# Decay and bonus rows on another queue, the bonus turned earlier, and two parts of the weights placed later on GpSimd

## The chip, the cores and the metric

One core of a Trainium2 chip. The metric is the device time of the whole kernel in microseconds, lower is better. A run counts as slow when it is over 1.5% above the fastest of the same kernel.

## The reference

An RWKV-style attention with decay `w` and bonus `u`, followed by a SiLU feed-forward over all tokens.

```python
# batch 4, heads 8, seq 768, head_dim 48
for t in range(S):
    cur = einsum('bhd,bhe->bhde', u[None] * kt, vt)
    y[:, :, t] = einsum('bhd,bhde->bhe', rt, state + cur)
    state = w[None, :, :, None] * state + einsum('bhd,bhe->bhde', kt, vt)
# x = y as 3072 x 384
h = x @ w_in              # 384 x 2048
g = h * (1 / (1 + exp(-h)))
return g @ w_out          # 2048 x 384
```

## The kernel before

The sequence is cut into chunks of 128 tokens. A unit is one chunk of one batch row, so there are 24 units. For each unit r and k are transposed and multiplied by powers of the decay ("rk"), their products give the scores ("ae", "ao"), masked on VectorE ("am"), and these with v give y. The bonus of a token is the row sum of r k u ("rku") times v ("vu"), added to y. The feed-forward products of one chunk ("hps", then "ops") fill TensorE between the units of the next. What the change touches is the start:

```python
    load_row(wrow, w)                           # on SP's queue
    load(0, mid=lambda: load_row(urow, u))      # u ahead of v of unit 0
    for i in range(1, B): load(i)
...
    spin(5)                                     # products on zeros, to raise TensorE's clock
    wT = to_cols(wrow, None)                    # the decay turned into a column
    spin(4)
    # ... powers of the decay on VectorE: pif
...
    p1(0, mid=to_cols_u)       # unit 0: transposes, rk; the bonus turned inside
    ...
    nc.gpsimd.tensor_copy(out=gate, in_=rin[1][:, 0, 0:1])   # GpSimd waits for r of unit 1
    win_part(0, 512)           # first quarter of w_in, GpSimd's queue
    nat_ku(0); nat_rk(0)       # GpSimd: k*u, r*k*u of unit 0
    p2(0)                      # scores of unit 0
    p1(1, spins=1)
    bonus_sum(0)               # VectorE: row sum rku
    nat_ku(1); nat_rk(1); nat_v(1)
    p3y(0)
    bonus_act(0)               # ScalarE: eight products vu
    ...
    win_part(512, 1024)
    bonus_sum(1); bonus_vu(1)
    p2(1, spins=2)
    p3e(0)                     # y16 = y + vu
    ...                        # two more quarters follow behind unit 2's bonus
```

Of the kernel before, what the change touches and what calls it, by code (L numbers as in the profile page):

```python
# [15 lines left out]
def kernel(  # L16
# [11 lines left out]
    nc = tc.nc  # L28

    B, H, S, D = r.shape  # L30
# [5 lines left out]
    PR = 64 + D  # L36
# [14 lines left out]
    rin = [big.tile([128, H, 64], FP, name=f"rin{i}") for i in range(NIN)]  # L51
    kin = [big.tile([128, H, 64], FP, name=f"kin{i}") for i in range(NIN)]
    vin = [big.tile([128, H, D], FP, name=f"vin{i}") for i in range(NIN)]
# [7 lines left out]
    def unit(i):  # L61
        return divmod(i, B)

    def load(i, mid=None):
        if i >= NU:
            return
        sc, b = unit(i)
        for t, src in ((rin, r), (kin, k), (vin, v)):
            if t is vin and mid:
                mid()  # L70
            nc.sync.dma_start(out=t[i % NIN][:, :, 0:D],
                              in_=src[b, :, sc * C:sc * C + C, :]
                              .rearrange("h t d -> t h d"))
# [4 lines left out]
    urow = cst.tile([NP, 2, 64], FP)  # L78
# [3 lines left out]
        nc.vector.memset(t[:, :, D:64], 1.0)  # L82

    def load_row(t, src):
        nc.sync.dma_start(out=t[:, :, 0:D], in_=bass.AP(tensor=src.tensor, offset=0,
                                                        ap=[[PW, NP], [D, 2], [1, D]]))

    load_row(wrow, w)
    load(0, mid=lambda: load_row(urow, u))
    for i in range(1, B):  # L90
        load(i)
    for t in (rin, kin):
        nc.vector.memset(t[0][:, :, D:64], 0.0)
# [6 lines left out]
        out=maskM, in_=maskM, compare_op=ALU.is_ge, fill=0.0,  # L100
# [17 lines left out]
    def spin(n, t=None):  # L118

        if t is None:  # L120
            t = ps.tile([128, 512], FP, name="spin", tag="t", bufs=5)
        else:
            t = t.rearrange("s p t -> s (p t)")
        for _ in range(n):
            nc.tensor.matmul(t, junk[:, 0:128], junk, start=True, stop=True)

    def to_cols(row, copy):
        t = ps.tile([128, 512], FP, name="cols", tag="t", bufs=5)
        nc.tensor.transpose(t[0:PR, 0:NP], row.rearrange("p j d -> p (j d)")[:, 0:PR],
                            ident[0:NP, 0:NP])  # L130
        if copy is None:
            return t[0:PR, 0:NP]
        c = cst.tile([PR, NP], FP, name="cols_sb")
        copy(out=c, in_=t[0:PR, 0:NP])
        return c

    spin(5)
    wT = to_cols(wrow, None)
    spin(4)
    u_bc = cst.tile([128, H, D], FP)  # L140
    lamC = cst.tile([128, H, D], FP)

    def to_rows(dst, cols):

        t = ps.tile([128, NP, 2, 64], FP, name="rows", tag="t", bufs=5)
        for p in range(NP):
            nc.tensor.transpose(t[:, p, :, :].rearrange("t j d -> t (j d)")[:, 0:PR],
                                cols(p), ident[0:PR, 0:PR])
        nc.scalar.copy(out=dst.rearrange("t (p j) d -> t p j d", j=2), in_=t[:, :, :, 0:D])


    nc.vector.tensor_copy(out=pi[:, 0:NP, 1:2], in_=wT.unsqueeze(2))
# [2 lines left out]
    while n < C:  # L155
        nc.vector.tensor_tensor(
            out=pi[:, :, 1 + n:1 + 2 * n], in0=pi[:, :, 1:1 + n],
# [14 lines left out]
    def nat_v(i):  # L172
        L = live.setdefault(i, {})
        L["v16"] = wrk.tile([128, H, D], F16, name="v16", bufs=6)
        nc.scalar.copy(out=L["v16"], in_=vin[i % NIN])

    def nat_ku(i):
        L = live.setdefault(i, {})
        L["ku"] = wrk.tile([128, H, D], FP, name="ku")
        nc.gpsimd.tensor_tensor(out=L["ku"], in0=kin[i % NIN][:, :, 0:D], in1=u_bc,  # L180
                                op=ALU.mult)

    def nat_rk(i):
        L = live[i]
        L["rku_f"] = wrk.tile([128, H, D], FP, name="rku_f")
        nc.gpsimd.tensor_tensor(out=L["rku_f"], in0=rin[i % NIN][:, :, 0:D], in1=L["ku"],  # L186
                                op=ALU.mult)
# [6 lines left out]
    def bonus_sum(i):  # L194
        L = live[i]
        L["rku"] = wrk.tile([128, H], FP, name="rku", bufs=3)
        nc.vector.tensor_reduce(out=L["rku"], in_=L["rku_f"], axis=mybir.AxisListType.X,  # L197
                                op=ALU.add)

    def bonus_vu(i):  # L200
        L = live[i]
        L["vu"] = wrk.tile([128, H, D], FP, name="vu", bufs=3)
        nc.gpsimd.tensor_tensor(out=L["vu"], in0=vin[i % NIN],  # L203
                                in1=L["rku"].unsqueeze(2).broadcast_to([128, H, D]),
                                op=ALU.mult)
# [5 lines left out]
            nc.scalar.activation(out=L["vu"][:, h, :], in_=vin[i % NIN][:, h, :],  # L211
                                 func=AF.Copy, scale=L["rku"][:, h:h + 1])

    def p1(i, mid=None, spins=0):
        n = i % NIN
        L = live.setdefault(i, {})
        tr = ps.tile([128, NP, C], FP, name="tr", tag="t", bufs=5)
        tk = ps.tile([128, NP, C], FP, name="tk", tag="t", bufs=5)
        spin(spins, tr)
        for t, src in ((tr, rin), (tk, kin)):  # L220
            flat = src[n].rearrange("p h d -> p (h d)")
            for p in range(NP):
                nc.tensor.transpose(t[0:PR, p, :], flat[:, 128 * p:128 * p + PR], ident)
        rk = wrk.tile([PR, 2, NP, C], FP, name="rk")
        L["rT"] = rk[:, 0]
        nc.vector.tensor_tensor(out=L["rT"], in0=tr[0:PR], in1=lamR, op=ALU.mult)
        if mid:
            mid()
        L["kT"] = rk[:, 1]
        nc.vector.tensor_tensor(out=L["kT"], in0=tk[0:PR], in1=lamK, op=ALU.mult)  # L230

    def p1t(i):

        n = i % NIN
        L = live.setdefault(i, {})
        xs = [ps.tile([128, 2, NP, 64], FP, name="xs", tag="t", bufs=5) for _ in range(2)]
        for a, src in enumerate((rin, kin)):
            flat = src[n].rearrange("p h d -> p (h d)")
            for p in range(NP):
                for g in range(2):  # L240
                    t = slice(64 * g, 64 * g + 64)
                    nc.tensor.transpose(xs[g][0:PR, a, p, :],  # L242
                                        flat[t, 128 * p:128 * p + PR], ident[t, t])
        rk = wrk.tile([PR, 2, NP, C], FP, name="rk")
        L["rT"] = rk[:, 0]
        L["kT"] = rk[:, 1]
        L["xs"] = xs, rk

    def p1d(i):
        L = live[i]  # L250
        xs, rk = L["xs"]
        for g in range(2):
            nc.vector.tensor_tensor(out=rk[:, :, :, 64 * g:64 * g + 64], in0=xs[g][0:PR],  # L253
                                    in1=lam(g), op=ALU.mult)
# [6 lines left out]
    def p2(i, spins=0, nxt=None, late=False):  # L261
        L = live[i]
        ae = ps.tile([128, NP, C], FP, name="ae", tag="t", bufs=5)
        ao = ps.tile([128, NP, C], FP, name="ao", tag="t", bufs=5)
        spin(spins, ae)
        for p in range(NP):
            nc.tensor.matmul(ae[:, p, :], L["kT"][0:D, p, :], L["rT"][0:D, p, :],  # L267
                             start=True, stop=True)
            nc.tensor.matmul(ao[:, p, :], L["kT"][64:PR, p, :], L["rT"][64:PR, p, :],  # L269
                             start=True, stop=True)  # L270
        if nxt is not None:
            p1t(nxt)
        L["am"] = []
        for a in (ae, ao):
            am = wrk.tile([128, NP, C], F16, name="am", bufs=4)
            nc.vector.tensor_tensor(out=am, in0=a,  # L276
                                    in1=maskM.unsqueeze(1).broadcast_to([128, NP, C]),
                                    op=ALU.mult)
            L["am"].append(am)
        if nxt is not None and not late:  # L280
            p1d(nxt)
# [15 lines left out]
    def p3e(i):  # L297
        L = live[i]
        L["y16"] = wrk.tile([128, H, D], F16, name="y16", bufs=3)
        nc.vector.tensor_tensor(out=L["y16"], in0=L["y"], in1=L["vu"], op=ALU.add)  # L300
# [105 lines left out]
            f()  # L406


    def to_cols_u():
        t = to_cols(urow, nc.scalar.copy)  # L410
        to_rows(u_bc, lambda p: t[:, p:p + 1].broadcast_to([PR, 128]))

    zero = junk[0:PR, 0:HD].rearrange("r (p c) -> r p c", p=NP)
    gate = cst.tile([128, 1], FP)

    def win_part(c0, c1):
        nc.gpsimd.dma_start(out=win[:, :, c0:c1],
                            in_=moe_w_in[:, c0:c1].rearrange("(q p) n -> p q n", p=128))
# [4 lines left out]
            in_=moe_w_out[1024 * g:1024 * g + 1024, :].rearrange("(f p) n -> p f n", p=128))  # L423


    p1(0, mid=to_cols_u)
    nat_v(0)
    lamCT = cst.tile([PR, NP, C], FP)
    for p in range(NP):
# [1 line left out]
                             scale=pi[:, p, C:C + 1])  # L431

    nc.scalar.copy(out=st[0], in_=zero)
    nc.gpsimd.tensor_copy(out=gate, in_=rin[1][:, 0, 0:1])
    win_part(0, 512)
    nat_ku(0)
    nat_rk(0)
    p2(0)
    p1(1, spins=1)
    bonus_sum(0)  # L440
# [4 lines left out]
    to_rows(lamC, lambda p: lamCT[:, p, :])  # L445
    bonus_act(0)
    nc.scalar.copy(out=st[1], in_=zero)
    win_part(512, 1024)
    bonus_sum(1)
    bonus_vu(1)  # L450
    p2(1, spins=2)
    p3e(0)
    spin(4)
# [183 lines left out]
```

## Time and profile before

| | before |
|---|---|
| median of the first 3 runs | 197.83 us (197.67 to 198.09) |
| the profiled execution | 197.53 us, span 195.8 us |
| TensorE busy | 188.7 us, 96% of the span |
| first feed-forward product (hps) | 16.80 us from the start |
| gaps of TensorE from 40 us to the last output | none to speak of |

A span runs from the first to the last instruction on the core; the device time is about 1.7 us longer. A line of the timeline has start, duration, engine, source line, operation, output and inputs; the bracket at its end tells how long the engine was idle before and which instruction released it. The lines themselves stand in the prediction.

### The profile page before, as it was taken

How to read it: one execution, taken by the hardware profiler on the slowest of the kernel's cores; microseconds unless marked ns; L12 is line 12 of the kernel's file. 1: busy time of each engine (PE TensorE's matmuls, PEld its weight loads, DVE VectorE, ACT ScalarE, POOL GpSimd, SP SyncE). 2: the span in 40 equal slices, each digit the busy share in tenths (PEclk: the TensorE clock that was granted, in tenths of full speed). 3: DMA queues.
4: the chain of work that ended last, by engine and by line, in shares of the span. 5: the costliest groups of instructions: out<-in, count | busy, mean ns of one | idle time of the engine just before them, and what ended most of it. 6: DMA issues, size and time to landing. Idle time of an engine off the chain costs nothing.

```text
span 195.8 us, 4923 instructions
## 1 busy us (share of the span) xinstructions
PE 188.7 (96%) x1919; PEld 126.9 (65%) x1919; DVE 115.4 (59%) x233; ACT 91.0 (46%) x207; POOL 115.2 (59%) x145
## 2 busy tenths in 40 slices
PE   7789999899999999999999999999999999999993
PEld 2657878787767887675657656557656556544563
DVE  6687658885857775975486676467566344210121
ACT  3655487799212534216871025692025680069300
POOL 4499959979975779678668737834537710000000
PEclk9999999999999999999999999999999999999999
DMA  4999998999893684476456377626551011210022
GB/s 85 215 187 169 196 205 175 183 190 204 167 218 104 158 177 88 100 174 154 90 107 127 110 177 159 127 40 122 128 155 44 20 22 44 93 48 0 3 82 80
DMA packets 89696, 24.12 MB, mean 123 GB/s; under 512 B 82888, under 2 KB 89672, under 8 KB 89672
## 3 DMA queue, kind: packets, MB, share of 16 engines
q1 hardware_dynamic: 85992, 20.66, 48.5%
q0 software_dynamic: 3680, 3.15, 10.7%
q8 instruction: 15, 0.25, 0.5%
q14 instruction: 9, 0.07, 0.1%
HBM read 20.45 MB, written 4.72 MB: 129 GB/s over the span
## 4 chain that ended last, share of the span: by engine, by line
PE 87%; DVE 4%; issue 4%; POOL 3%; ACT 0%; POOLq 0%; DVEq 0%
PE ops L370 31%; PE hps L358 31%; PE ae L267 11%; PE xs L242 4%; PE y L293 3%; DVE am L276 2%; PE y L290 2%; PE sps L309 2%; PE ops L384 1%; POOL rku_f L186 1%; POOL ku L180 1%; PE yT L346 1%; PE ao L269 1%; DVE y L300 1%; DVE rku L197 1%
## 5 line engine op out<-in xcount | busy, mean ns | idle before, releaser
L361 ACT ACTIVATE gT<-hps 128x256 f16<-128x256 f32 (+1 forms) x128 | 59.8, 494 | 50.5 <-PE hps L358 48.9
L358 PE MATMUL hps<-xT,win 128*128 128x256 f16 (+1 forms) x384 | 69.2, 326 | 0.2
L370 PE MATMUL ops<-wout,gT 128*128 128x384 f16 x368 | 63.8, 326 | 0.0
L358 PEld LDWEIGHTS <-win 128*128 128x128 f16 x384 | 35.4, 98 | 22.9 <-issue 0.8
L370 PEld LDWEIGHTS <-gT 128*128 128x128 f16 x368 | 34.7, 98 | 22.4
L276 DVE TENSOR_TENSOR am<-ae,maskM 128x512 f16<-128x512 f32 x24 | 16.6, 692 | 33.5 <-PE ao L269 33.4
L374 DVE COPY osb<-ops 128x384 f32<-128x384 f32 x23 | 12.8, 555 | 28.8 <-PE ops L370 28.7
L267 PE MATMUL ae<-rk 48*128 48x128 f32 x192 | 27.7, 285 | 1.0 <-DVE rk L230 1.0
L267 PEld LDWEIGHTS ae<-rk 48*128 48x128 f32 x192 | 23.1, 187 | 8.5 <-issue 4.7
L269 PE MATMUL ao<-rk 48*128 48x128 f32 x192 | 27.7, 285 | 0.0
L203 POOL TENSOR_TENSOR vu<-vin,rku 128x384 f32<-128x384 f32 x23 | 19.1, 832 | 14.1 <-DVE rku L197 14.0
L259 ACT CAST rT<-rk 112x512 f16<-112x512 f32 x20 | 12.3, 616 | 31.8 <-DVE rk L253 31.8
L253 DVE TENSOR_TENSOR rk<-xs,pif 112x512 f32<-112x512 f32 x40 | 25.6, 681 | 1.7 <-PE xs L242 1.7
L180 POOL TENSOR_TENSOR ku<-kin,u_bc 128x384 f32<-128x384 f32 x24 | 24.1, 1006 | 2.1 <-DMA kin<-in_k_dram 2.1
L186 POOL TENSOR_TENSOR rku_f<-rin,ku 128x384 f32<-128x384 f32 x24 | 24.1, 1004 | 1.9
L191 POOL TENSOR_TENSOR kc<-kin,lamC 128x384 f16<-128x384 f32 x24 | 24.0, 1003 | 0.0
L269 PEld LDWEIGHTS ao<-rk 48*128 48x128 f32 x192 | 23.1, 187 | 0.0
L323 POOL CAST stb<-st 112x384 f16<-112x384 f32 x12 | 6.1, 505 | 20.4 <-DVE st L318 20.4
L300 DVE TENSOR_TENSOR y<-y,vu 128x384 f16<-128x384 f32 x24 | 13.4, 557 | 7.6 <-PE y L293 2.2
L276 DVE TENSOR_TENSOR am<-ao,maskM 128x512 f16<-128x512 f32 x24 | 16.3, 681 | 0.0
L197 DVE TENSOR_REDUCE rku<-rku_f 128x8 f32<-128x384 f32 x24 | 13.2, 550 | 1.8 <-POOL rku_f L186 1.3
L325 POOL TENSOR_TENSOR sdec<-st,pif 112x384 f32<-112x384 f32 x16 | 13.4, 838 | 1.1 <-ACT gT L361 1.1
(74 smaller groups left out, 168.5 us busy)
## 6 DMA issues: line engine op xcount, KB each, us to landing
rin<-in_r_dram SPq DMA_DIRECT2D x24, 192.0 KB, 2.9
kin<-in_k_dram SPq DMA_DIRECT2D x24, 192.0 KB, 3.5
vin<-in_v_dram SPq DMA_DIRECT2D x24, 192.0 KB, 3.7
out_dram<-osb SPq DMA_DIRECT2D x23, 192.0 KB, 1.9
win<-in_moe_w_in_dram POOLq DMA_DIRECT2D x4, 384.0 KB, 6.0
wout<-in_moe_w_out_dram POOLq DMA_DIRECT2D x2, 768.0 KB, 9.8
xT<-y SPq DMA_TRANSPOSE x18, 2.3
out_dram<-osh SPq DMA_DIRECT2D x1, 128.0 KB
```

What stands on the lines that cost most here:

```text
L180: nc.gpsimd.tensor_tensor(out=L["ku"], in0=kin[i % NIN][:, :, 0:D], in1=u_bc, op=ALU.mult)
L186: nc.gpsimd.tensor_tensor(out=L["rku_f"], in0=rin[i % NIN][:, :, 0:D], in1=L["ku"], op=ALU.mult)
L191: nc.gpsimd.tensor_tensor(out=kc[i % NKC][:, :, 0:D], in0=kin[n][:, :, 0:D], in1=lamC, op=ALU.mult)
L203: nc.gpsimd.tensor_tensor(out=L["vu"], in0=vin[i % NIN], in1=L["rku"].unsqueeze(2).broadcast_to([128, H, D]), op=ALU.mult)
L253: nc.vector.tensor_tensor(out=rk[:, :, :, 64 * g:64 * g + 64], in0=xs[g][0:PR], in1=lam(g), op=ALU.mult)
L267: nc.tensor.matmul(ae[:, p, :], L["kT"][0:D, p, :], L["rT"][0:D, p, :], start=True, stop=True)
L269: nc.tensor.matmul(ao[:, p, :], L["kT"][64:PR, p, :], L["rT"][64:PR, p, :], start=True, stop=True)
L276: nc.vector.tensor_tensor(out=am, in0=a, in1=maskM.unsqueeze(1).broadcast_to([128, NP, C]), op=ALU.mult)
L300: nc.vector.tensor_tensor(out=L["y16"], in0=L["y"], in1=L["vu"], op=ALU.add)
L358: nc.tensor.matmul(hps, win[:, q, ft * 128:(ft + 1) * 128], xts[sc][:, q, b0:b1, :].rearrange("p b t -> p (b t)"), start=(q == 0), stop=(q ...
L361: nc.scalar.activation(out=gts[sc][:, ft, b0 * C:b1 * C], in_=hps, func=AF.Silu)
L370: nc.tensor.matmul(ops, gts[sc][:, ft, b * C:(b + 1) * C], wout[:, ft, :], start=(ft == 0), stop=(ft == NFT - 1))
```

## The change

Its intent: r and k of unit 0 no longer queue behind the row of w, nor v of unit 0 and all later inputs behind both rows; GpSimd no longer waits for r of unit 1 before the bonus of unit 0; the weights stop competing with the first inputs.

```diff
-        nc.sync.dma_start(out=t[:, :, 0:D], in_=bass.AP(tensor=src.tensor, ...
+        nc.scalar.dma_start(out=t[:, :, 0:D], in_=bass.AP(tensor=src.tensor, ...
     load_row(wrow, w)
-    load(0, mid=lambda: load_row(urow, u))
-    for i in range(1, B):
+    load_row(urow, u)
+    for i in range(B):
         load(i)
...
-    spin(5)
+    spin(6)
     wT = to_cols(wrow, None)
-    spin(4)
+    spin(1)
+    ucol = to_cols(urow, nc.scalar.copy)
+    spin(2)
...
+    to_rows(u_bc, lambda p: ucol[:, p:p + 1].broadcast_to([PR, 128]))
...
-    p1(0, mid=to_cols_u)
+    p1(0)
...
+    nat_ku(0)
+    nat_rk(0)
     nc.gpsimd.tensor_copy(out=gate, in_=rin[1][:, 0, 0:1])
     win_part(0, 512)
-    nat_ku(0)
-    nat_rk(0)
...
-    win_part(512, 1024)
     bonus_sum(1)
     bonus_vu(1)
+    nc.gpsimd.tensor_copy(out=gate, in_=rin[2][:, 0, 0:1])
+    win_part(512, 1024)
```

More of the change, by code (lines that the diff above doesn't have):

```diff
@@ L62, in unit, with load @@
         return divmod(i, B)
-    def load(i, mid=None):
+    def load(i):
         if i >= NU:
@@ L68, in load @@
         for t, src in ((rin, r), (kin, k), (vin, v)):
-            if t is vin and mid:
-                mid()
             nc.sync.dma_start(out=t[i % NIN][:, :, 0:D],
@@ L84, in load_row @@
     def load_row(t, src):
-        nc.sync.dma_start(out=t[:, :, 0:D], in_=bass.AP(tensor=src.tensor, offset=0,
+        nc.scalar.dma_start(out=t[:, :, 0:D], in_=bass.AP(tensor=src.tensor, offset=0,
                                                         ap=[[PW, NP], [D, 2], [1, D]]))
     load_row(wrow, w)
-    load(0, mid=lambda: load_row(urow, u))
-    for i in range(1, B):
+    load_row(urow, u)
+    for i in range(B):
         load(i)
@@ L212, in bonus_act, with p1 @@
                                  func=AF.Copy, scale=L["rku"][:, h:h + 1])
-    def p1(i, mid=None, spins=0):
+    def p1(i, spins=0):
         n = i % NIN
@@ L226, in p1 @@
         nc.vector.tensor_tensor(out=L["rT"], in0=tr[0:PR], in1=lamR, op=ALU.mult)
-        if mid:
-            mid()
         L["kT"] = rk[:, 1]
@@ L406, in fill @@
             f()
-    def to_cols_u():
-        t = to_cols(urow, nc.scalar.copy)
-        to_rows(u_bc, lambda p: t[:, p:p + 1].broadcast_to([PR, 128]))
     zero = junk[0:PR, 0:HD].rearrange("r (p c) -> r p c", p=NP)
```

## The prediction

> **What bounds the kernel now.** I read the page first (busy times, then the 40 slices), then the chain of waits for its first 40 us, then the timeline of the first 28 us, then single tiles for DMA landings.
>
> The page: TensorE is busy 188.7 of 195.8 us.
>
> ```profile
> PE 188.7 (96%) x1919; PEld 126.9 (65%) x1919; DVE 115.4 (59%) x233; ACT 91.0 (46%) x207; POOL 115.2 (59%) x145
> PE   7789999899999999999999999999999999999993
> DMA  4999998999893684476456377626551011210022
> ```
>
> From about 40 us (slice 8) TensorE has no gap to the end, so what the change does must be seen in its start, and any shift there reaches the end unchanged. The first 17 us are a prologue: much of TensorE's work there is "spin" products on zeros, and the first feed-forward product ("hps") starts at 16.80 us. So I ask what sets 16.80, and which waits follow up to 40 us.
>
> The chain of waits (start, duration, what):
>
> ```profile
> 2.74 4.55 issue
> 7.31 0.19 POOL gate L434
> 7.54 0.85 issue
> 8.39 1.03 POOL ku L180
> 9.49 1.00 POOL rku_f L186
> 10.49 0.96 POOL ku L180
> 11.54 1.02 POOL rku_f L186
> 12.58 0.55 DVE rku L197
> 13.13 1.21 DVE am L276 x2
> ```
>
> GpSimd stands still for 4.6 us until r of unit 1 lands (the gate), issues the first weights (0.85), and only then makes unit 0's and unit 1's bonus products. They feed the row sum of unit 1 on VectorE, which feeds the masked scores "am" and, after 16 us, hps. The change takes the gate out of this chain. But the chain names only the last of several near-equal paths; the timeline gives the others:
>
> ```profile
> 3.50 0.25 PE L129 MATMUL cols<-ident,wrow 4*112 4x4 f32 x1
> 4.08 2.38 DVE L156 TENSOR_TENSOR pif<-pif 112x8 f32<-112x8 f32 x7
> 6.60 0.69 DVE L226 TENSOR_TENSOR rk<-tr,pif 112x512 f32<-112x512 f32 x1
> 11.54 0.54 DVE L197 TENSOR_REDUCE rku<-rku_f 128x8 f32<-128x384 f32 x1
> 12.12 1.91 ACT L211 ACTIVATE vu<-vin,rku 128x48 f32<-128x48 f32 x8 [0.34 <-DVE rku L197]
> 12.58 0.55 DVE L197 TENSOR_REDUCE rku<-rku_f 128x8 f32<-128x384 f32 x1 [0.50 <-POOL rku_f L186]
> 14.24 1.15 DVE L300 TENSOR_TENSOR y<-y,vu 128x384 f16<-128x384 f32 x2
> ```
>
> The reader is to see two things. VectorE waits on GpSimd only 0.50 us in this stretch; that is all the gate costs directly. And a second path, decay row turned (3.50), powers of the decay (to 6.46), unit 0, unit 1, row sum of unit 0 (12.08), ScalarE's eight bonus products (to 14.03), ends only about 0.15 us before y of unit 0 begins at 14.24 (14.03 and some 0.05 of signalling make 14.08).
>
> **What the Trainium skill says.** "Trainium Kernel Development and Optimization", Key Constraints: DMAs of the SP, ACT and POOL queues run on the same 16 DMA engines, and issuing from several saves issue time only. The trace agrees that issue time is what is at stake: the two rows hold SP's queue for 0.84 and 0.67 us (first r is issued at 1.71), while the engines are near fully busy from 3 us on. "Perfetto Trace Analysis", Summary: the profiler window per engine type: a DMA's record on SP is descriptor generation, not movement. It agrees: r of unit 1 has a record of 0.58 us from 3.98 and lands 3.3 us after its issue, at the 7.31 of the gate. "ScalarE: Activation LUTs", What ACT_TABLE_LOAD costs: 1283 ns for the load; the trace has 1.28 us at 0.80. "TensorE: Matmul & The Clock Gate", Part 1: the clock is halved until some 3.4 us of activity have passed. The first spins start 0.42 us apart, and one at 14.73 takes 0.22, so an added early spin costs the long time.
>
> **The change part by part.**
>
> 1. Rows to ScalarE's queue. SP loses 0.84 + 0.67 us of issue. r of unit 0 moves from 1.71 to about 0.81, so all inputs are issued 0.9 us earlier, those behind u up to 1.5. Unit 0's r and k landed at 4.4 and 5.1 (issue plus 2.7 and 2.9) and are multiplied at 6.60, after the powers of the decay. They are not on the path: worth 0. ScalarE issues both rows from 0.80, so its table load moves from 0.80 to about 2.3 and its first small activation from 2.10 to about 3.6. Its next work was at 6.15. Hidden.
>
> 2. spin(5) becomes spin(6) ahead of the decay's turn. Five spins end in issue at 1.26 + 5 x 0.42 = 3.4 and the turn came at 3.50; six end at 3.8. This is on the path: decay powers, unit 0's products and everything behind on VectorE move by **+0.3 us**, more if the w row lands later beside r. The other spins fall from 4 to 1 + 2, so their sum stays nine.
>
> 3. Bonus turned in front of unit 0. TensorE: turn at about 4.5, ScalarE's small copy (0.16), four row transposes (0.6) to about 5.7, ScalarE's copy (0.48) to about 6.3, where the trace has 7.48. So u_bc is ready some 1.1 us earlier. Unit 0's transposes move behind it, about 5.7 to 6.6, still ahead of the decay powers (now about 6.8). Hidden.
>
> 4. First weights behind unit 0's products. GpSimd: ku of 0 from 6.3, rku_f from 7.35 to 8.35, gate 0.19, issue 0.94 to 9.4, ku and rku_f of unit 1 to about 11.5, where the trace has 12.55. VectorE's wait of 0.50 goes. It now comes: am of unit 0 at 9.44 (+0.3), unit 1, row sum 0 to 12.38 (+0.3), row sum 1 to 12.9, am of unit 1 12.9 to 14.15 (before: 13.05 to 14.32), so **-0.15**. But ScalarE's bonus products follow row sum 0: 12.42 + 1.91 = 14.33, and y of unit 0 begins at about 14.38 in place of 14.24. **Net +0.15 at the first hps.** Even without the extra spin this path allows y only at 14.08, a gain of 0.16.
>
> 5. Second weights. They were issued at 12.48, while GpSimd had nothing else to do until row sum 1 (13.13): free. Now they stand behind the bonus of unit 1: vu from 12.95 to 13.8, gate 0.2, issue 0.8 to 14.7. So ku of unit 2 starts at 14.7, not 14.10: **+0.6 us** on a queue that is full to 24 us. Weights 3 and 4 move from 17.09 to about 17.7, and the loads of unit 4 behind them as much. Who needs these? Weights 4 landed at 25.0 (17.87 plus 7.1), and their first use on TensorE is the hps at 25.12. A landing at 25.6 against a use at 25.12 + 0.15 is a new TensorE stall of 0.35. Weights 3 (landing 22.8, use 23.5) have slack enough for 0.6; weights 1 (landing about 14.8, use 16.3) and 2 (about 19.5, use 20.7) too. k of unit 4 goes from 26.4 to 27.0, with its use moved likewise.
>
> Sum: +0.15 + 0.35 = **+0.5 us**. On 197.83 that is 198.3. I state 198.2, because earlier input issue empties the DMA queue sooner and may let weights 4 land with less queueing.
>
> **Rivals.**
>
> A: the gate's chain is all that counts, and its removal pays in full. If row sum 1 set everything, the gain is the 0.50 us wait, some 197.3; with 0.9 us of earlier transfers added, 196.9. For it: the chain of waits says so. Against it: the ScalarE bonus path, 0.15 us behind.
>
> B: the weights become the bound. Their landing times are 5.7 to 7.1 us after issue, and two of four uses come within a microsecond of landing. If each of three later parts slips by 1 us instead of 0.6, stalls of 1 us follow: 198.8 to 199.2. For it: the slack of weights 4 is 0.1 us. Against it: the inputs, which competed (k of unit 3 took 8.4 us), are now issued earlier and are nearly done by then.
>
> C: the w row comes late through ScalarE. If its table load is placed ahead of the rows, w lands 1.3 us later and the decay powers with it: about 199.2. Against it: the rows come first in the program, and the trace ascribes the load to the Silu behind them.
>
> D: everything is hidden in the prologue: 197.8.
>
> **Range and chances.** B and C are the upper edge, 199.3; A the lower, 197.0. Two per cent is 4.0 us, more than half of all TensorE idle time (195.8 - 188.7 = 7.1 us, most of it ahead of 17 us), and no path I found is worth a third of it in either direction. So within 2% has 0.97, slower 0.02, faster 0.01.
>
> **What would show it.** In the changed trace: decay turn at about 3.8 and the first rk product at about 6.9 (step 2); ku of unit 0 at about 6.3 (3); no VectorE wait at row sum 1, y of unit 0 at about 14.4 set by ScalarE's vu (4); ku of unit 2 at about 14.7, weights 3 issued at about 17.7, a TensorE wait of some 0.3 us ahead of the hps near 25.3 (5). From 40 us on, the same work without gaps, shifted by the sum. Wrong it would be if the w row landed before 3.4 and the clock rose early, so that the powers start no later; if weights 4 land no later than 25.0; or if first hps moves by over 0.3 us either way.

## The result and the profile after

The changed kernel takes 197.78 us (median of 6 runs, 197.77 to 197.84); the kernel before took 197.96 us (197.67 to 198.34, 6 runs) on the same chip. The ratio is 0.999, with a 95% interval of 0.9978 to 1.0003: the same. A ratio here is the mean time of one kernel's fast runs over that of the other's of the same rounds, so it is not quite the ratio of the medians quoted.

The profiled executions say a little more: 197.53 us before, 197.78 after, spans of 195.8 and 196.1. **In these two traces the changed kernel is 0.25 us slower**, while its median is not. Both facts need a cause.

From the page of the changed kernel, the busy times, then TensorE and DMA in 40 slices of the span:

```profile
PE 188.3 (96%) x1919; PEld 126.9 (65%) x1919; DVE 115.5 (59%) x233; ACT 91.3 (47%) x207; POOL 115.6 (59%) x146
...
PE   6689999999999999999999999999999999999993
...
DMA  6998998999795774477456387616561011210022
```

The same work (GpSimd has one instruction more, the second gate), the same nearly full TensorE from slice 3 on (counted from 0, so from 15 us). The DMA engines are busier in the first slice (6 tenths against 4) and less so around 15 to 20 us.

From its chain of waits (start, duration, what):

```profile
1.26 2.74 PE spin L123 x6
4.00 0.18 PE cols L127
...
6.18 0.70 DVE pif L158
7.01 0.69 DVE rk L228
...
8.36 0.37 PE ae L267
9.57 1.28 DVE am L276 x2
...
12.10 0.36 PE ae L267
13.30 1.28 DVE am L276 x2
```

GpSimd is gone from the chain. It now starts with the six spins and runs through the decay's turn, the powers, unit 0, and unit 1's scores on TensorE, which release "am" at 13.30. From its timeline, the lines that answer those of before:

```profile
3.93 0.23 PE L127 MATMUL cols<-ident,wrow 4*112 4x4 f32 x1
4.10 0.39 PE L123 MATMUL spin<-junk 128*128 128x512 f16 x1
...
11.95 1.00 DVE L199 TENSOR_REDUCE rku<-rku_f 128x8 f32<-128x384 f32 x2
...
12.53 1.92 ACT L213 ACTIVATE vu<-vin,rku 128x48 f32<-128x48 f32 x8 [0.34 <-DVE rku L199]
...
13.28 0.69 DVE L276 TENSOR_TENSOR am<-ae,maskM 128x512 f16<-128x512 f32 x1 [0.33 <-PE ao L269]
...
14.49 1.15 DVE L300 TENSOR_TENSOR y<-y,vu 128x384 f16<-128x384 f32 x2
```

The turn comes at 3.93 instead of 3.50. Both row sums now follow each other with no wait, where the second had waited 0.50 us for GpSimd; "am" behind them now waits 0.33 us for TensorE instead. y of unit 0 starts at 14.49 instead of 14.24, and the first hps at 17.04 instead of 16.80. From there on the two traces run in step, 0.25 us apart.

The weights' landing, by the view of the tile that holds them: first the third and fourth part in the kernel before, then in the changed one. The first line of each has the durations of issue and the first and last start; the second the time from issue to landing.

```profile
L417 POOL DMA_DIRECT2D win<-in_moe_w_in_dram x2: 775/790/804, 17.1 to 17.9; - x2
...
DMA to landing us min/median/max: 5.7/6.4/7.1
```

```profile
L413 POOL DMA_DIRECT2D win<-in_moe_w_in_dram x2: 775/790/804, 17.7 to 18.5; - x2
...
DMA to landing us min/median/max: 5.0/5.7/6.4
```

They are issued 0.65 us later and take 0.7 us less, so part 4 lands at about 25 us in both. TensorE takes it up at 25.4 now, without a wait.

### The profile page after: what moved, and what is told of

Its sections match the earlier page's. It is cut to its first block, busy times and chain, and to the rows that moved or that the text cites. A ratio compares the mean times of both kernels' runs of the same rounds, so it can differ in the third digit from the quotient of the medians.

```text
span 196.1 us, 4922 instructions
## 1 busy us (share of the span) xinstructions
PE 188.3 (96%) x1919; PEld 126.9 (65%) x1919; DVE 115.5 (59%) x233; ACT 91.3 (47%) x207; POOL 115.6 (59%) x146
## 4 chain that ended last, share of the span: by engine, by line
PE 90%; DVE 6%; issue 1%; ACT 0%; DVEq 0%
PE ops L370 31%; PE hps L358 31%; PE ae L267 12%; PE xs L242 4%; PE y L293 3%; DVE am L276 3%; PE y L290 2%; PE sps L309 2%; PE spin L123 2%; PE ops L384 1%; DVE pif L158 1%; PE ao L269 1%; PE yT L346 1%; DVE y L300 1%; ACT xT L347 0%
```

## The experiments

All kernels gave correct results. The first four ran on one chip, with 5 to 6 timed runs each and the kernel before beside them (11 runs). No ratio below reaches 2%, the size that counts as faster or slower; where a kernel is called slower or better all the same, its 95% interval leaves out 1. "Undone" means relative to the changed kernel.

**Is the sixth spin the delay?** My theory was yes (S); the rival was a late w row (W).

```diff
-    spin(6)
+    spin(5)
     wT = to_cols(wrow, None)
```

> The changed kernel with five spin products ahead of the decay's turn in place of six. In the profile of the changed kernel the turn came at 3.93 us (3.50 before) and the first hps at 17.04 (16.80 before). Theory S (the sixth spin is the delay): turn at about 3.6, the powers of the decay, unit 0's products and the first hps 0.3 us earlier (hps at about 16.7), span about 195.8. Rival W (the w row lands late through the ScalarE queue, beside the first r): turn stays at 3.8 to 3.9, hps at 17.0, span 196.1. In both the timed runs should agree within 0.1 us, as those of the changed kernel do (197.77 to 197.84), if the place of the weights is what steadies it.

Measured: 200.75 us (199.29 to 201.46), ratio 1.0141, interval 1.0113 to 1.0168. Neither theory gave that. The turn itself came at 3.58, as S says, so w lands in time and the sixth spin does hold it back. But then the timeline of TensorE shows:

```profile
5.51 0.22 PE L127 MATMUL cols<-ident,urow 4*112 4x4 f32 x1 [1.16 <-DMA urow<-in_u_dram]
...
7.24 1.06 PE L225 MATMUL tr<-ident,rin 128*112 128x128 f32 x4
...
12.35 1.06 PE L225 MATMUL tr<-ident,rin 128*112 128x128 f32 x4
...
14.30 0.58 PE L147 MATMUL rows<-ident,lamCT 112*128 112x112 f32 x4
```

u came only at about 5.37, TensorE stood idle 1.16 us for it, and then the four transposes took 1.06 us where they take 0.60 in the kernel before and the changed one. The products run at half speed until about 14 us. Such doubled durations of equal products are the mark of the start-up clock that the prediction named in its citation of "TensorE: Matmul & The Clock Gate", Part 1, and then used only to price one spin. The first hps came at 20.20, 3.2 us late, and the profiled run took 200.92, 3.1 us more than the changed kernel's. The same page says of the window in which activity is measured that it is "free-running" and does not begin with the kernel; the traces below agree that the rise has no fixed time.

**Does ScalarE's queue bring anything?** The rows back on SP's queue, the rest as changed.

```diff
-        nc.scalar.dma_start(out=t[:, :, 0:D], ...
+        nc.sync.dma_start(out=t[:, :, 0:D], ...       # w first, u ahead of v of unit 0
```

> The changed kernel with the two rows back on SP's queue (w first, u ahead of v of unit 0), all else as changed; six spins. If ScalarE's queue brings nothing to the end (my step 1): turn of the decay at 3.9 as the sixth spin sets it, hps within 0.15 us of 17.04, span 196.0 to 196.2; u lands at about 5.0 in place of 4.6, so its turn and the bonus row come some 0.3 to 0.6 us later and ku of unit 0 with them, hidden. Rival (earlier inputs do matter): unit 0's transposes or the row sums come later, hps at 17.4 or more. Spread of the timed runs: under 0.1 us if the weights' place alone steadies the kernel, 0.5 us or more if the issue of the rows does.

Measured: 200.35 us, six runs from 197.78 to 201.74, three of them slow by the 1.5% rule, ratio of the fast ones 1.0057, interval 1.002 to 1.0095. The profile fell on the 197.78: turn of the decay at 3.93, turn of u at 5.35 after 0.63 us of idle time, span 196.1. So in the good case the queue is worth nothing, as step 1 said. Five of the six runs were 1.5 to 4.0 us slower, where the changed kernel has none above 198.1; what the queue is worth there no profile shows. This variant keeps the weights in their new places and spreads by 4 us.

**The weights in their old places**, the rest as changed (gate and first part ahead of unit 0's bonus, second part ahead of row sum 1, no second gate):

```diff
+    gate(rin[1]); win_part(0, 512)
     nat_ku(0); nat_rk(0)
-    gate(rin[1]); win_part(0, 512)
...
+    win_part(512, 1024)
     bonus_sum(1); bonus_vu(1)
-    gate(rin[2]); win_part(512, 1024)
```

> The changed kernel with the weights in their old places: gate and first part ahead of ku of unit 0, second part ahead of the row sum of unit 1, no second gate. Rows on ScalarE and bonus turned in front stay. GpSimd's gate ends at about 6.5 (r of unit 1 lands at 6.4) instead of 7.5, so ku of unit 0 runs at about 7.5 and row sum 1 no longer waits by much: hps at about 17.0, span 195.9 to 196.2. Spread of the timed runs is the question: kernel before has 197.67 to 198.34 in six runs, changed 197.77 to 197.84. Theory T (weights queued among the inputs make the runs differ): 0.4 us or more between lowest and highest here, median about 198.0. Rival R (row issue or the turn order): spread under 0.15 us, median 197.8.

Measured: 198.5 us; three runs at 197.77 to 197.87 and three at 199.13 to 199.25. The spread that T asked for is there, but the profile, of a run at 199.22, gives another reason. TensorE's timeline:

```profile
4.11 0.61 PE L123 MATMUL spin<-junk 128*128 128x512 f16 x1
5.40 0.22 PE L127 MATMUL cols<-ident,urow 4*112 4x4 f32 x1 [0.68 <-DVE pif L158]
...
7.13 1.06 PE L225 MATMUL tr<-ident,rin 128*112 128x128 f32 x4
...
9.83 0.37 PE L267 MATMUL ae<-rk 48*128 48x128 f32 x1 [0.78 <-DVE rk L230]
```

The turn of u again late, the transposes slow, the clock up only by 9.83. The first hps is at 18.52, 1.5 us late: all of the difference. This program issues the same instructions on every engine as the changed kernel until past 6 us, so the weights can't have caused the late turn at 5.40. The trace puts this wait down to a VectorE product done long before ("pif"); that u was late is inferred. And TensorE was slow before it: the single spin at 4.11 takes 0.61 us, where the same one at 4.10 in the changed kernel takes 0.39.

**The weights' move alone**, on the kernel before.

> The kernel before with the weights' move alone (first part and its gate behind unit 0's two bonus products, second part behind unit 1's bonus behind a gate on r of unit 2); rows on SP, five spins, bonus turned in the middle of unit 0. u_bc is ready at 7.48, so ku of unit 0 starts at about 7.5 in place of 8.39 and the wait at row sum 1 (0.50 us) goes, but ScalarE's bonus path caps the gain at 0.16: hps 16.65 to 16.8, span 195.6 to 195.9. Theory T: spread of the timed runs under 0.15 us, median 197.4 to 197.6. Rival R: spread stays 0.5 us, median about 197.9.

Measured: 198.28 us (197.78 to 198.84), ratio 1.003, interval 1.0012 to 1.0047. Slower by 0.3%, where I had expected a gain of up to 0.16 us. The profiled run (197.78) has the clock up as early as the kernel before. What went wrong is on VectorE:

```profile
12.83 0.55 DVE L197 TENSOR_REDUCE rku<-rku_f 128x8 f32<-128x384 f32 x1 [0.75 <-POOL rku_f L186]
```

The wait at row sum 1 grew from 0.50 to 0.75 us. I had counted that unit 0's bonus starts earlier and forgotten that gate and issue (0.19 and 0.93 us) only move from ahead of unit 0 to ahead of unit 1, and row sum 1 waits for unit 1. Without the earlier u_bc of the other part, unit 1's bonus is done at 12.80, later than the 12.55 of before. First hps comes at 17.05, 0.25 us later than before, which is nearly the whole gap between the fastest runs (197.78 and 197.51). The move needs the early turn of the bonus beside it. Why other runs of this variant reach 198.84 no profile shows.

**The changed kernel again**, to see whether it too has late clocks.

> The changed kernel unaltered, timed again beside the others. Theory H (start-up clock): whether TensorE's clock doubles at about 4.3 us or only at 9 to 14 us depends on how long TensorE stands idle for the u row, and that differs from run to run; the run with weights in the old place, which is the same program up to 6 us, gave 197.8 three times and 199.2 three times. Then the changed kernel too must show runs at 197.8 and runs at 199 or more among six, median above 198. Rival T (the new place of the weights steadies the kernel): all six within 0.15 us of 197.8, as on the day of the prediction.

Measured: 197.78 us, five runs at 197.76, 197.76, 197.78, 198.09 and 198.10; ratio 1.0005, interval 0.9993 to 1.0017. My theory H asked for runs at 199 and fell here. With the first six, eleven runs lie within 0.35 us. In both its profiles the turn of u came early (4.71 and 4.57). The second, of the run at 198.09, also shows where its 0.3 us went: first hps is at 17.05 as ever, but later TensorE waits for the second half of w_out, 768 KB issued at 37.8 that took 13.0 us to land (11.7 in the first profile):

```profile
50.79 2.11 PE L370 MATMUL ops<-wout,gT 128*128 128x384 f16 x12 [0.28 <-DMA wout<-in_moe_w_out_dram]
```

So not every run some tenths above the fastest is a matter of the start.

**More spins**, three instead of one ahead of u's turn and three ahead of unit 0's scores; once on the changed kernel, once with the weights in their old places.

```diff
-    spin(1)
+    spin(3)
     ucol = to_cols(urow, nc.scalar.copy)
...
-    p2(0)
+    p2(0, spins=3)
```

> The changed kernel with three spins in place of one between the turns of w and u, and three more between unit 0's transposes and its first product, where TensorE stood idle (4.5 to 4.7, up to 5.4 when u is late; 6.7 to 8.4). No work is added to the path if the clock is up. Theory H: TensorE is busy without a gap from 1.26 to beyond 8, so the clock rises in every run at 4.3 to 5 us: six runs within 0.3 us, 197.7 to 198.0, and no run at 199. Rival U (the late landing of u itself costs the time, not the clock): the spins change nothing, runs of 199 and more stay.

> The same added spins with the weights in their old places (gate and first part ahead of unit 0's bonus, second part ahead of row sum 1). Theory H: no run at 199; the run without these spins had its fast half at 197.8. GpSimd's second product of unit 1 is done by 11.7 here against 11.94, and y of unit 0 is set by ScalarE's bonus path in both, so the head is the same within 0.1 us: 197.7 to 197.9. Rival T: spread of 0.4 us or more, as the weights lie among the inputs.

Measured: 198.23 us (197.76 to 198.91) and 198.12 us (197.76 to 198.68), ratios 1.0024 and 1.0019. No run at 199 any more, but half of the runs of each between 198.2 and 198.9. The first of the two has the weights in their new places and still spreads over 1.15 us: **T is refuted: the weights' new places are not enough to steady a kernel.** In the profile of the second (198.28) three spins ahead of u take 1.46 us and the two behind it 0.93, so the clock rose only at about 6.3, and the first hps is at 17.57. Spins that run at half speed are themselves on the path.

**u first on SP's queue**, w alone on ScalarE's, so that u can't be late.

```diff
     load_row(wrow, w)                # ScalarE's queue
-    load_row(urow, u)                # ScalarE's queue
+    load_row(urow, u, nc.sync)       # ahead of r of unit 0
```

> The changed kernel with the u row first on SP's queue (ahead of r of unit 0) and w alone on ScalarE's. So far the turn of u came at 4.6 us in the two profiles of the changed kernel and at 5.3 to 5.5 in four others that issue u behind w or among the inputs, and where it came late TensorE stood idle 0.5 to 1.2 us ahead of it. Theory H2 (a late u leaves that gap, and then the clock may rise late): u lands at about 3.6, its turn follows w's at about 4.5 without a wait, and all runs are at 197.7 to 198.1. r of unit 0 is issued at about 1.7 as in the kernel before and lands by 4.5, ahead of its transposes. Rival: the late rise comes from where the start falls in a free-running window; then runs above 198.5 appear here too.

> The same with five spins ahead of the turn of w and two behind it, nine in all as before. With six, the changed kernel lost 0.4 us at the turn (3.93 against 3.50); with five and u late it lost 3 us to the slow clock. Theory S with H2: turn at 3.5, powers of the decay 0.4 us earlier, unit 0's products at about 7.95, first hps at 16.65 to 16.75, span 195.7, time 197.4, no run above 198. If the sixth spin is needed for the clock whether u is late or not: runs at 199 or more.

> The weights in their old places with rows and bonus turn as changed (three of six runs were at 199.2), now with u first on SP's queue. This tells the two causes of the slow runs apart. Theory H2: no run above 198.2, as u is no longer late. Rival T (the weights' new place is what steadies the changed kernel): again runs above 198.7.

Measured, with six spins: 197.77, 197.77, 197.85, 198.61, 198.78 and one slow run of 386.46, which by ill luck was the profiled one. With five: 197.75 us, runs at 197.35 to 197.47 three times and 198.02 to 198.26 three times, ratio 0.9993. With the weights in their old places: 198.18 us, 197.77 to 198.22, ratio 1.0008; the runs at 199 of that order did not come back.

So H2 is half right, and its rival, which asked for runs above 198.5 here too, got two of them (198.78 and 198.61, not profiled). The second of these kernels, profiled in a run at 198.26, shows that u's turn no longer waits, that five spins do bring the decay's turn to 3.51, and that the clock was late all the same; it rose between these two groups of transposes:

```profile
6.41 1.01 PE L225 MATMUL tr<-ident,rin 128*112 128x128 f32 x4
7.26 0.60 PE L225 MATMUL tk<-ident,kin 128*112 128x128 f32 x4
```

The three fast runs of the five-spin kernel are 0.3 to 0.4 us below the fastest with six spins beside it (197.77). That fits theory S, that this is what the sixth spin costs when the clock is early; none of the three was profiled.

**When the clock rose** can be read from the traces, which keep the clock's own record. It begins at the rise; the granted clock printed with a run counts the time before it as full, so a late start does not show in it.

| profiled run | full clock from, us | TensorE idle ahead of u's turn, us | time, us |
|---|---|---|---|
| before | 4.47 | u turned later | 197.53 |
| changed, its two profiles | 4.02, 4.26 | 0.22, none | 197.78, 198.09 |
| the weights' move alone | 4.41 | u turned later | 197.78 |
| more spins | 4.15 | 0.47 | 197.79 |
| rows on SP's queue | 5.16 | 0.63 | 197.78 |
| old places, more spins | 6.38 | none | 198.28 |
| old places, u first | 7.13 | none | 198.21 |
| u first, five spins | 7.25 | none | 198.26 |
| old places | 8.94 | 0.68 | 199.22 |
| five spins | 14.13 | 1.16 | 200.92 |

The two kernels of the next part have 5.02 and 4.24. The stretch of full clock that follows lasts 191.146 us in eleven of the thirteen traces, 187.733 with the weights in their old places and 184.320 with five spins: steps of 3.413 us. So the clock seems to be decided at the ends of windows of that length. Counted back from the rise, TensorE was busy for 2.76 us or more in the window just before each rise, as the profile counts it, and for 2.73 us or less in every earlier window; no trace differs. With five spins, the window with the 1.16 us of waiting had 2.25 us of work and its neighbours 2.63 each; with old places, the one with 0.68 us of waiting had 2.73; on SP's queue the 0.63 us of waiting still left 2.97, and the clock rose. In the three late cases without a wait, the window that ended at 2.96 to 3.83 had begun well before the first spin at 1.26 and held only 1.70 to 2.57 us of work; the rise came one window later. As far as these traces show, two things decide: where the start falls in the windows, which differs from run to run, and whether TensorE idles inside one. H2 has the second, its rival the first. No experiment set the place of the windows; this is read from one profile of each variant, two of the changed kernel.

The slow run is a picture of its own. From the page of that execution and TensorE's timeline:

```profile
PE 379.7 (99%) x1919; PEld 206.6 (54%) x1919; DVE 116.7 (30%) x233; ACT 96.1 (25%) x207; POOL 115.2 (30%) x146
```

```profile
6.43 1.16 PE L225 MATMUL tr<-ident,rin 128*112 128x128 f32 x4
```

VectorE and GpSimd do their work in the same time as ever (116.7 and 115.2 us); TensorE's took twice as long to the end. The granted clock was printed as 1.00, but this is no measurement: the trace holds no record of the clock at all, where each of the thirteen others holds one from the rise on. One of the runs of the kernel before took 321.12 us, with a granted clock of 0.564, so long executions are not peculiar to the variant. What held the clock back in these two is not known.

**A version that beats both.** In the changed kernel VectorE stands idle from 8.30 to 9.57 while TensorE makes unit 0's scores, and TensorE from 6.7 to 8.4. Unit 1's r and k have landed by then, so its transposes and VectorE products go in front of unit 0's scores (cut to what matters here):

```diff
-    p2(0)
-    p1(1, spins=1)
-    bonus_sum(0)
+    p1(1)
+    bonus_sum(0)
+    p2(0)
     nat_ku(1); nat_rk(1); nat_v(1)
-    p3y(0)
-    to_rows(lamC, ...)
     bonus_act(0)
+    win_part(512, 1024)              # weights in their old places
     bonus_sum(1); bonus_vu(1)
-    p2(1, spins=2)
+    p2(1)
+    p3y(0)
+    to_rows(lamC, ...)
```

> A version meant to beat both: rows and bonus turn as changed, three spins ahead of u's turn, weights in the old places, and unit 1's transposes and VectorE products moved in front of unit 0's score products, so that VectorE works while TensorE makes them (it waited 1.2 us there, 8.3 to 9.57) and unit 1's scores follow at once; row sum 0 and ScalarE's bonus products start some 2 us earlier. By my reckoning am of unit 1 ends at about 13.4 instead of 14.6, first hps at 16.0 to 16.2 instead of 17.04, all later issues of weights about 0.9 us earlier: 196.9 to 197.2 if the weights land as much earlier, 197.4 to 197.7 if weights 4 (used 0.1 us after landing in the kernel before) now make TensorE wait.

Measured: 196.96 us (196.92 to 197.30, 5 runs), ratio 0.9963, interval 0.995 to 0.9976. From its timeline:

```profile
8.24 0.68 DVE L228 TENSOR_TENSOR rk<-tr,pif 112x512 f32<-112x512 f32 x1
...
12.48 0.68 DVE L276 TENSOR_TENSOR am<-ae,maskM 128x512 f16<-128x512 f32 x1
...
16.23 0.49 PE L358 MATMUL hps<-xT,win 128*128 128x256 f16 x3
```

Unit 1's rk now fills the idle stretch, am of unit 1 begins at 12.48 instead of 13.30, and the first hps is 0.8 us earlier than in the changed kernel. No weight makes TensorE wait. Beside the lines shown, this version has three spins ahead of u's turn, two fewer ahead of unit 1's y, and the first weights ahead of unit 0's bonus. The parts were not varied one by one; the interval of the whole leaves out 1, but the gain of 0.4% is under the 2% that count.

The last kernel adds u first on SP's queue, five spins (two ahead of u's turn in place of three), four spins ahead of unit 1's transposes, and unit 0's bonus ahead of the gate and the first weights, as the change has it:

> The best version so far (unit 1 in front of unit 0's scores, 196.96) with u first on SP's queue, five spins, unit 0's bonus ahead of the gate and the first weights, and four spins ahead of unit 1's transposes for the wait until r and k of unit 1 land (7.3 and 8.1). u_bc at about 5.8, unit 0's bonus done by 7.9, row sum 0 no longer waits for GpSimd (0.45 us there); unit 0's products at about 8.6, am of unit 1 done at about 13.2 instead of 13.76, first hps at 15.6 to 15.8 instead of 16.23, time 196.4 to 196.6. If k of unit 1 lands later than 8.1, or the weights make TensorE wait at the later parts, 196.9 or more.

Measured: 196.96 us (196.53 to 197.21, 6 runs), ratio 0.9952, interval 0.9934 to 0.997. Its best runs are 0.4 us below those of the version above, with the first hps at 15.78 in the profiled one (196.53), but half of its runs lie at 197.1 to 197.2. The medians do not differ; it is not shown to be the better of the two.

## Why the prediction was right, and where its steps were not

The stated time was 198.2 us in a range of 197.0 to 199.3, and 197.78 was measured; "within 2%" was right. By its steps:

1. **Rows by ScalarE's queue: right, hidden.** r of unit 0 is issued at 0.81. w's record on ScalarE is 1.26 us rather than the 0.84 it had on SP, which puts the table load at 2.77 rather than 2.3, still hidden. Not foreseen: u, queued behind w and beside r and k, is turned at 4.57 or 4.71 in some profiles and at 5.40 to 5.51 in others.
2. **Sixth spin: right in kind, a little too small.** The turn moved by 0.43 us, not 0.3, and the first rk product to 7.01 (6.9 was stated). Taking the spin away alone gave the turn at 3.58. What the step did not see is that a spin is also work for the clock: without it, and with u late, the clock rose only at 14.13.
3. **Bonus turned in front: right.** ku of unit 0 starts at 6.42 (6.3 stated). It took 1.31 us instead of 1.03, so GpSimd had unit 1's products done at 11.94, not 11.5; still in time.
4. **First weights behind unit 0: right that VectorE's wait of 0.50 goes and nothing is gained.** y of unit 0 starts at 14.49 (14.38 stated). But the size came partly from another place: am of unit 1 did not move ahead by 0.15 us, since it waits for TensorE's scores of unit 1 until 13.30. That path, which follows the decay's turn, I had not written down; with it the first hps comes 0.24 us later, not 0.15. It was there to read: before the change the last score of unit 1 ends at 12.84 (12.57 plus 0.27), only 0.2 us ahead of am at 13.05, so the wait of 0.50 could give back no more than that; and 12.84 plus the 0.43 of the sixth spin is 13.27, where am now starts at 13.28. ScalarE's vu ends close by, at 14.45 against 14.57 for am, so the trace does not tell which of the two holds y. The sentence that row sum 1 "feeds" am is wrong too: am does not read it, it only stands behind it on VectorE.
5. **Second weights: issue times right, stall wrong.** ku of unit 2 began at 14.75 (14.7 stated), parts 3 and 4 were issued 0.65 us later (0.6 stated). The stall of 0.35 us did not come: I had added the old time to landing to the new issue time. It is 5.0 and 6.4 us where it was 5.7 and 7.1. My remark that emptier queues may help was right and should have been the estimate. That these two parts land earlier after issue because the inputs have drained is an argument from the DMA slices; no run varied it by itself, and part 2, also issued later, took 6.0 us instead of 5.7.

The sum of the steps was +0.5 us; the traces show +0.25. The fastest timed runs agree with the traces: 197.76 for the changed kernel (11 runs) against 197.51 for the one before (38 runs without the one at 321). That the medians are nevertheless equal comes from the kernel before, which rarely runs at its fastest: its runs go from 197.51 to 198.68 with a median of 197.85. A late rise of the clock was seen in five profiled variants, and a wait of 0.28 us for w_out in one run of the changed kernel; for the kernel before itself none of its longer runs was profiled, so which of the two it is stays open.

Rival A (the gate's removal pays in full) is refuted by the changed trace: GpSimd left the chain and the first hps came later. That holds without the sixth spin too: the kernel with u first and five spins has its fastest run 0.19 us below the fastest of the kernel before in its call (197.35 and 197.54), not 0.50, though it also has u on another queue. B and C did not occur. D, nothing moves, is nearest for the median, though not for its reason: a loss of 0.25 us in the best case and fewer of the longer runs cancel.

**What stays open:** why the changed kernel's eleven runs cost at most 0.35 us more than the fastest, while the variant with the same first 6 us had three of six at 199.2. Its two profiles show u early and the rise at 4.02 and 4.26; why u is late in some runs no run shows. With the rows back on SP's queue the times spread by 4 us, with five spins by 2 us, both with the weights in their new places: these places are not enough. That they do nothing is not shown.

## What to carry to other kernels

When the chain of waits names one path, write down the two or three that end within a few tenths of it before pricing its removal; here GpSimd's wait of 4.6 us gave way to one of 3.7 us for the bonus row, unit 0's products came 2 us earlier, and of that some 0.2 us could reach the end. A landing time is not issue plus a constant: if the issue moves to where the queue is emptier, the landing may not move. And small waits of TensorE in the first microseconds can go with a loss much longer than themselves, through the clock (3.1 us beside a wait of 1.16), or with none (beside one of 0.63), so look at the duration of equal products early in the trace, in several runs, before moving anything there.

## What the Trainium skill lacked or had wrong

- "TensorE: Matmul & The Clock Gate", Part 1, puts the ramp penalty at under 1% of a typical kernel span. Here the late rise cost about 1.6% (200.92 us in the profiled five-spin run against 197.78 for the changed kernel), and the rise came at 4.0 to 14.1 us over variants that differ in one spin or one row's queue.
- No page that I read warns that a granted clock worked out from the clock's records counts the time before the first record as full: 0.998 was printed for the run with 1.06 us for four transposes (0.60 otherwise), whose record begins at 14.13 us, and 1.00 for a whole execution of 386.46 us that has no record.
- No page tells how much idle time a window may hold for the clock still to rise at its end: here 2.76 us of work in 3.41 were enough and 2.73 were not.
- An execution at half speed to its end (386.46 us) is covered at most by the first page's remark that the monitor has been seen stuck.
- "DMA: Bandwidth & Descriptors", Anatomy of one DMA — SWDGE (gpsimd) path, fits 2.0 us plus bytes over 436 GB/s, an estimate of 2.9 us for a part of 384 KB. Under this kernel's other traffic the parts took 4.8 to 7.1 us from issue to landing in the fast profiled runs.
